# Attention and a gated feed-forward layer on one core: w_out of the first tile loaded and multiplied by column halves

## The chip, the cores and the metric

One core of a Trainium2 chip runs the whole program. The metric is device time in microseconds (us); lower is better. The core has five engines that run beside each other, each through its own instructions in order: TensorE (PE) multiplies, VectorE (DVE) and ScalarE (ACT) do elementwise work and empty PSUM, GpSimd (POOL) works on SBUF only, and SyncE (SP) mostly issues loads. ACT and POOL can issue transfers too. All transfers are carried by 16 DMA engines. Matmul results land in PSUM, which has eight banks of 512 float32 columns on 128 partitions.

## The reference

Blockwise causal attention over 8 batches, 8 heads, 576 positions and head size 64, then a gated feed-forward layer over the 4608 tokens:

```
mask = pos[:, None] // 64 >= pos[None, :] // 64
scores = np.where(mask, q @ k.T / 8, -1e9)
attn = softmax(scores) @ v                       # q, k, v: (8, 8, 576, 64)
x = attn.transpose(0, 2, 1, 3).reshape(4608, 512)
out = (np.maximum(x @ w_gate, 0) * (x @ w_val)) @ w_out   # 512 -> 1536 -> 512
```

The inputs are float32; the kernel multiplies in bfloat16 and gives float32.

## The kernel before, in words

**Tiles.** The feed-forward layer runs in nine tiles of 512 tokens: tile j below 8 is the first 512 positions of batch j, and tile 8 gathers the last 64 positions of all batches. A tile has an up part (gate and value products against `wg` and `wv`, each kept as three blocks of 512 hidden columns; relu on ACT; the product `hT` on DVE) and an output part (`hT` against `wo`). Tiles 0 and 1 take the plain output: four groups of 128 tokens, each 12 matmuls of 512 columns (`out_mm`). Later tiles use a scheme of seven products per 2x2 block (`seven_products`, matmuls of 256 columns).

**Attention.** A pair of heads is a round r = 4 b + hp. Each round has named steps: `s` the scores (`visit`, two double banks "sc" and two single banks of `thirds`) with their first exponentials on ACT, `e` the last exponential, `c` the corners (`corners`: memsets that zero what the block mask forbids), `a` and `b` the products with v of its two heads (`head_av`, with the division on DVE), and `x` the transposes into the tile's input xT. Before that, batch 1's q and k are cast (`q4`, `q6` for heads 4 to 7) and transposed on PE (`m0` to `m3`, `mains_1`). Batch 0 has its own form: `p` (a part of the scores with its exponential), `M` (transposes of q and k), `c0` to `c3b`, `a`, `b`, `x`.

**Order.** The order is written out by hand. `ffn_gen` is a generator that yields after each of the feed-forward layer's matmuls (or pairs of them); the table `AT` gives each other step a place, counted in those yields. Places 0 to 96 are tile 0's up part, 96 to 144 its output part, 144 begins tile 1. Steps are issued in the order of their places, and every engine then runs its share in that order. `HOW` says which engine or PSUM bank a step uses. Loads with places below those of their casts go to SP's queue in the same order: `w00` to `w21` load w_out, `cw..` cast it on POOL; `E1v0` loads v of heads 0 to 3 of batch 1 (casts `ev0a`, `ev0b`), `E1v4` that of heads 4 to 7 (cast `ev4`, L223), `E1q4` and `E1q6` its q and k; `T0`, `E2q0` and later ones follow. A load needs a free one of ten "stage" buffers, each of 4 KB on a partition. The casts turn float32 into bfloat16.

**PSUM.** "sc" has two double banks, "one" a single bank, "ffnp" three banks; a buffer is taken again when its reader is done. In tile 0's output part the four groups rotate through the "ffnp" banks. Each result is copied to an "ob" buffer on DVE (L1191), and its store is kept for later (`late`, issued at steps `o0` to `o3`).

Of the kernel before, what the change touches and what calls it, by code (L numbers as in the profile page):

```python
# [10 lines left out]
FP = mybir.dt.float32  # L11
BF = mybir.dt.bfloat16
# [5 lines left out]
def kernel(  # L18
# [10 lines left out]
    nc = tc.nc  # L29
# [17 lines left out]
    sb = ctx.enter_context(tc.tile_pool(name="sb", bufs=1))  # L47
# [320 lines left out]
    def load_w(dst, view):  # L368

        st = new_stage(1024).rearrange("p (c n) -> p c n", c=dst.shape[1])  # L370
        nc.sync.dma_start(st, view.rearrange("(c p) f -> p c f", p=128))
        return dst, st
# [14 lines left out]
        )  # L387

    def load_w_out(i, g):
        return load_w(  # L390
            wo[i][:, 2 * g : 2 * g + 2],
            moe_w_out[512 * i + 256 * g : 512 * i + 256 * g + 256],
        )

    def cast_w(w, eng, rows=slice(None)):
        dst, st = w
# [36 lines left out]
    def head_of(hh):  # L433
        return slice(64 * hh, 64 * hh + 64)

    def thirds():
        return (
            psum_one.tile([128, 512], FP, name="one"),
            psum_ffn.tile([128, 512], FP, name="ffnp"),
        )  # L440

    def visit(r):

        b, hp = divmod(r, 4)
        at = attnT[r % 4]
        first = psum_sc.tile([128, 2, 512], FP, name="sc")
        second = psum_sc.tile([128, 2, 512], FP, name="sc")
        third = thirds()
        tails = b >= FIRST
        pieces = [(2, False), *((c, True) for c in range(4) if tails)]  # L450
        for c, tail in pieces + [(c, False) for c in (0, 1, 3)]:
            for hh in range(2):
                where = {
                    0: first[:, hh, :],
                    1: second[:, hh, 0:384],
                    3: second[:, hh, 384:512],
                    2: third[hh][:, 0:256],
                }
                if tail:
                    o = third[hh][:, 256 + 64 * c : 320 + 64 * c]  # L460
# [481 lines left out]
    def ffn_gen():  # L942
        for j in range(B + 1):
# [245 lines left out]
            def finish(op, s, n0, n1):  # L1189
                ob = sb.tile([128, 512], FP, name="ob", bufs=5)[:, 0 : n1 - n0]  # L1190
                nc.vector.tensor_copy(ob, op)  # L1191
                if store:
                    store.pop()()
                (store if j else late).append(lambda j=j: put(j, s, ob, n0, n1))

            if j >= SEVEN:
                sums.step(12)
                yield from seven_products(j, quads, sums)
                continue

            groups = outs(j)
            while groups:
                some = 2 if j == 0 and len(groups) == 4 else 1
                ops = [
                    psum_ffn.tile([128, 512], FP, name="ffnp")[:, 0 : n1 - n0]
                    for _, n0, n1 in groups[:some]
                ]
                for f0 in (0, 4, 8) if some == 2 else (0,):
                    for op, (s, n0, n1) in zip(ops, groups):
                        for f in range(f0, f0 + 4 if some == 2 else 12):  # L1210
                            out_mm(op, s, f, n0, n1)
                            if f == 11:
                                finish(op, s, n0, n1)
                            yield
                groups = groups[some:]

    def outs(j):
        full = [(s, 0, 512) for s in range(4)]
        return full if j < B else full[:3] + [(3, 0, 352), (3, 352, 512)]
# [26 lines left out]
    with tc.manual_schedule(engines={E.PE, E.DVE, E.Activation, E.Pool, E.SP}):  # L1246
# [81 lines left out]

        def mains_1(hp):
            engs, banks = HOW[f"m{hp}"]  # L1330
            if banks == "one":
                both = bank("one", BF)
# [5 lines left out]
        AT = {  # L1338
            "p00": -41,
            "p02": -40.5,  # L1340
            "cq4": -40,
# [10 lines left out]
            "p12": -34.5,  # L1352
            "j2": -34,
            "M3q": -33.5,
            "M3k": -33,
            "cv0": -32.5,
            "cv2": -32,
            "c1": -31.5,
            "p20": -31,
            "a0": -30.5,  # L1360
            "p21": -30,
            "b0": -29.5,
# [4 lines left out]
            "x0": -27,  # L1367
            "cv00/01": -26.5,
            "cv00/23": -26,
            "cg00/01": -25.5,  # L1370
            "p30": -25,
            "cv4a": -24.5,
            "cv4b": -24,
            "cg00/23": -23.5,
            "x1": -23,
            "p32": -22.5,
            "c2": -22,
            "c3a": -21.5,
            "c3b": -21,
            "cv6a": -20.5,  # L1380
            "a2": 3,
            "b2": 3.01,
            "cv6b": 3.02,
            "C1": 3.03,
            "a3": 6,
            "b3": 6.01,
            "x2": 6.02,
            "x3": 8,
            "g01": -53.5,
            "v01": -53.4,  # L1390
# [16 lines left out]
            "cv20": 31,  # L1407
            "cg21": 31.91,
            "cv21/0": 32.24,
            "ev0a": 32.33,  # L1410
            "ev0b": 32.34,
            "Lq0": -63.5,
            "Lq2": -62.27,
            "Lv0": -61.59,
# [12 lines left out]
            "j1": -41.2,  # L1427
            "j4": -41.17,
            "E1q0": 20.29,
            "w01": 32.1,  # L1430
            "w00": 32.11,
            "w11": 32.11,
            "w20": 32.12,
            "w10": 32.12,
            "E1v0": 32.16,
            "w21": 32.16,
            "E1q6": 32.19,
            "E1q4": 32.19,
# [5 lines left out]
            "cw00": 32.3,  # L1444
            "cw10": 32.3,
            "cw01": 32.3,
            "cw21/0": 32.33,
            "cw11": 32.33,
            "cw20": 32.33,
            "q6": 32.36,  # L1450
            "q4": 32.36,
            "E2q4": 33.82,
            "ev4": 34.05,
            "tc0": 34.05,
# [5 lines left out]
            "m1": 87.1,  # L1460
            "s4": 95,
            "E2v0": 109.09,
            "cw21/1": 110.84,
            "e4": 114.3,
            "c4": 116.83,
            "s5": 119.48,
            "a4": 120.37,
            "b4": 120.57,
            "e5": 121.28,
            "m2": 122.6,  # L1470
            "c5": 124.67,
            "E2v4": 125.35,
            "T2": 126.26,
            "a5": 127.05,
            "s6": 128.09,
            "e6": 128.35,
            "b5": 129.8,
            "c6": 131.42,
            "m3": 132.5,
            "x4": 135.4,  # L1480
            "x5": 135.8,
            "s7": 139.49,
            "a6": 139.55,
            "b6": 140.59,
            "e7": 141.27,
            "c7": 141.68,
            "x6": 145.48,
            "a7": 147.62,
            "b7": 147.81,
            "x7": 153,  # L1490
            "td0": 156.81,
            "t0": 163.43,
            "td1": 157,
# [89 lines left out]
            "t1": ("dve", "dve"),  # L1583
            "m0": (("act", "dve"), "one"),
            "m1": (("dve", "act"), ("sc", "ffn")),
            "m2": (("act", "act"), ("sc", "ffn")),
            "m3": (("act", "act"), "one"),
            "u0": ("pool", "pool"),
            "u3": ("dve", "act"),
            "r4": ("dve", "one", "ffn", ("act", "sc")),  # L1590
            "r5": ("dve", "ffn", "ffn", ("act", "ffn")),
            "r6": ("dve", "ffn", "ffn", ("act", "sc")),
            "r7": ("dve", "sc", "one", ("dve", "one")),
# [9 lines left out]
            "cw21/1": "dve",  # L1603
            "cv00/01": "pool",
            "cg01/01": "pool",
            "c0": "dve",
            "c1": "dve",
            "c2": "dve",
            "c3a": "dve",
            "c3b": "dve",  # L1610
            "M1": ("dve", "dve"),
            "M2": ("dve", "dve"),
            "M3": ("dve", "dve"),
# [7 lines left out]
            "cw21/0": "pool",  # L1621
            "cg00/01": "pool",
            "cg00/23": "pool",
            "cg01/23": "act",
# [21 lines left out]
                "c" + n: piece(n)  # L1646
                for n in (
                    "g00/01 g00/23 v00/01 v00/23 g01/01 g01/23 v01 g10 v10 g11 v11 "
                    "g20 v20 g21 v21/0 v21/1 w00 w01 w10 w11 w20 w21/0 w21/1"
                ).split()  # L1650
            },
            "C0": lambda: constants(0, nc.vector),
# [162 lines left out]
```

## Time and profile before

| | us |
|---|---|
| median of 3 runs (351.25 to 351.93) | 351.65 |
| the profiled execution | 352.3 |
| its span, first to last instruction | 350.5 |
| PE busy | 339.8 (97%) |
| DVE, ACT, POOL busy | 225.5, 185.2, 153.8 |
| granted TensorE clock | 0.999 |

The rest of the profile is read in the prediction. A group or timeline row gives the start, the busy time, the engine, the line of the kernel, the operation, out<-in with shapes, and in brackets how long the engine stood idle before it and what released it. "SPq" or "ACTq" is an engine's sequencer, which issues transfers. The chain of waits goes back from the last instruction, at each step to what released it. A table by stage gives the engines' busy times, the clock, the share of time that a DMA engine moved data (packets that overlap can bring it over 1), and GB/s.

### The profile page before, as it was taken

What the parts mean: (1) busy time and instruction counts of PE and PEld (TensorE: products, weight loads), DVE (VectorE), ACT (ScalarE), POOL (GpSimd) and SP (SyncE); (2) the same over time, 40 slices, a digit from 0 to 9 for tenths busy, and PEclk for the clock granted to TensorE, in tenths of its full rate; (3) what the DMA queues carried; (4) which work ended last, traced back from release to release, by engine and by line L of the source; (5) the groups of instructions that cost most, each with busy time, mean ns of one, the idle gap of its engine ahead of it and who ended that gap; (6) DMA issues with size and microseconds to landing.
All of it is one profiled execution on the core that took longest, in us unless ns stands there. A gap on an engine that the chain in (4) does not pass through costs nothing.

```text
span 350.5 us, 8275 instructions
## 1 busy us (share of the span) xinstructions
PE 339.8 (97%) x3210; PEld 208.2 (59%) x3254; DVE 225.5 (64%) x564; ACT 185.2 (53%) x297; POOL 153.8 (44%) x194
## 2 busy tenths in 40 slices
PE   8999999999999999999999999999999999999994
PEld 3544455545445568545855576556755687687673
DVE  4853455667529784467547772668567867986892
ACT  5933766687235862666355545555366525423521
POOL 2767556576598902590149203950300022213213
PEclk9999999999999999999999999999999999999999
DMA  8999989999999994999459974999510031003005
GB/s 240 295 353 373 352 224 248 222 148 155 184 185 153 144 182 98 138 147 169 62 134 141 104 135 123 127 131 150 121 47 17 16 94 50 2 2 121 1 2 120
DMA packets 155399, 50.02 MB, mean 143 GB/s; under 512 B 134464, under 2 KB 151744, under 8 KB 155360
## 3 DMA queue, kind: packets, MB, share of 16 engines
q0 software_dynamic: 70528, 8.98, 49.1%
q1 hardware_dynamic: 77520, 32.52, 44.0%
q10 hardware_dynamic: 7312, 8.00, 7.8%
q8 instruction: 25, 0.41, 0.5%
q14 instruction: 14, 0.11, 0.1%
HBM read 37.75 MB, written 9.44 MB: 135 GB/s over the span
## 4 chain that ended last, share of the span: by engine, by line
PE 77%; DMA 14%; POOL 3%; issue 2%; DVE 2%; ACT 1%; SPq 1%; POOLq 0%; ACTq 0%
PE ffnp L948 39%; PE ffnp L830 12%; PE one L830 5%; PE sc L1014 3%; DMA stage<-in_moe_w_out_dram 3%; PE sc L465 3%; DMA xT<-xnat 2%; DMA stage<-in_moe_w_val_dram 2%; PE one L465 2%; DMA stage<-in_v_dram 2%; DMA stage<-in_moe_w_gate_dram 2%; PE ffnp L600 2%; PE one L600 2%; PE ffnp L1181 2%; PE one L1014 2%
## 5 line engine op out<-in xcount | busy, mean ns | idle before, releaser
L958 ACT ACTIVATE gate_sb<-ffnp 128x512 bf16<-128x512 f32 x95 | 57.1, 605 | 74.8 <-PE ffnp L948 66.5
L948 PE MATMUL ffnp<-xT,wg 128*128 128x512 bf16 x338 | 93.0, 379 | 1.7 <-issue 0.6
L948 PE MATMUL ffnp<-xT,wv 128*128 128x512 bf16 x309 | 87.7, 380 | 1.0 <-DVE hT L968 0.3
L968 DVE TENSOR_TENSOR hT<-gate_sb,ffnp 128x512 bf16<-128x512 bf16 x76 | 51.9, 683 | 46.0 <-PE ffnp L948 27.0
L948 PEld LDWEIGHTS <-wv 128*128 128x128 bf16 x384 | 35.4, 98 | 38.2 <-issue 4.6
L470 ACT ACTIVATE attnT<-sc 128x1024 bf16<-128x1024 f32 x56 | 57.0, 1042 | 0.0
L948 PEld LDWEIGHTS <-wg 128*128 128x128 bf16 x384 | 35.7, 98 | 35.0 <-issue 1.7
L882 POOL TENSOR_TENSOR ob<-ob 128x512 f32<-128x512 f32 x7 | 9.6, 1370 | 101.7 <-ACT ob L879 53.3
L830 PEld LDWEIGHTS <-stage 128*128 128x128 bf16 x420 | 40.3, 98 | 6.0
L789 DVE TENSOR_TENSOR stage<-hT 128x512 bf16<-128x512 bf16 (+2 forms) x82 | 37.8, 493 | 0.9
L600 PEld LDWEIGHTS <-attnT 128*128 128x128 bf16 x640 | 26.7, 98 | 11.9 <-DVE attnT L1241 0.9
L830 PE MATMUL ffnp<-stage 128*128 128x256 bf16 x252 | 31.4, 273 | 0.0
L353 POOL DMA_DIRECT2D v_bf<-in_v_dram x30 | 24.1, 869 | 6.1 <-DVE recip L537 2.6
L477 ACT ACTIVATE attnT<-one 128x512 bf16<-128x512 f32 (+1 forms) x28 | 15.0, 536 | 21.1 <-PE ffnp L465 21.1
L353 POOL DMA_DIRECT2D q_bf<-in_q_dram x20 | 17.9, 907 | 16.7 <-DVE hT L968 9.7
L1181 PE MATMUL ffnp<-wo,hT 128*128 128x512 bf16 x91 | 23.2, 379 | 0.3
L465 PEld LDWEIGHTS <-kTm 64*128 64x128 bf16 x384 | 11.0, 94 | 15.1 <-issue 7.9
L1045 POOL TENSOR_TENSOR ob<-ob 128x512 f32<-128x512 f32 x6 | 7.6, 1266 | 23.2 <-ACT ob L1044 23.2
L353 POOL DMA_DIRECT2D k_bf<-in_k_dram x20 | 17.8, 927 | 0.0
L830 PEld LDWEIGHTS <-hT 128*128 128x128 bf16 x168 | 16.4, 98 | 1.9
L465 PE MATMUL sc<-qTm,kTm 64*128 64x512 bf16 (+1 forms) x168 | 16.8, 305 | 0.0
L879 ACT COPY ob<-ffnp 128x512 f32<-128x512 f32 x7 | 4.1, 585 | 22.1 <-PE ffnp L830 22.1
(194 smaller groups left out, 556.0 us busy)
## 6 DMA issues: line engine op xcount, KB each, us to landing
out_dram<-ob ACTq DMA_DIRECT2D x28, 256.0 KB, 2.3
stage<-in_moe_w_val_dram SPq DMA_DIRECT2D x6, 512.0 KB, 8.7
stage<-in_moe_w_gate_dram SPq DMA_DIRECT2D x6, 512.0 KB, 8.2
stage<-in_moe_w_out_dram SPq DMA_DIRECT2D x6, 512.0 KB, 10.5
q_bf<-in_q_dram POOLq DMA_DIRECT2D x20, 128.0 KB, 4.2
k_bf<-in_k_dram POOLq DMA_DIRECT2D x20, 128.0 KB, 5.2
v_bf<-in_v_dram POOLq DMA_DIRECT2D x20, 128.0 KB, 7.0
stage<-in_v_dram SPq DMA_DIRECT2D x19, 128.0 KB, 5.5
```

The source lines that it names most:

```text
L353: ins = nc.gpsimd.dma_start(dst, part_of)
L465: nc.tensor.matmul(o, kTm[b % 2][head_of(hh), c, hp, :], qT, start=True, stop=True)
L470: return lambda: nc.scalar.activation(at[:, :, lo : lo + 512], sc, AF.Exp, scale=scale)
L477: nc.scalar.activation(at[:, hh, 1024 : 1024 + w], third[hh][:, 0:w], AF.Exp, scale=scale)
L600: nc.tensor.matmul(av[:, p, :], at[:, col : col + 128], v_bf[b % 2][:, c, h, :], start=(p == 0), stop=(c == p), skip_group_check=True,)
L789: nc.vector.tensor_tensor(out=out.rearrange("p (c n) -> p c n", c=m), in0=a, in1=b, op=op)
L830: nc.tensor.matmul(to, sums.of(c)[which][:, 128 * p : 128 * p + 128], right, start=first, stop=(c == 5), skip_group_check=True,)
L948: nc.tensor.matmul(to, (wg, wv)[t][f // 4][:, c, 128 * (f % 4) : 128 * (f % 4) + 128], x[:, c], start=(c == 0), stop=(c == 3),)
L958: nc.scalar.activation(gate_sb, gate, AF.Relu)
L968: nc.vector.tensor_tensor(out=h, in0=gate_sb, in1=val, op=AX.mult)
L1014: nc.tensor.matmul(to[:, 256 * k : 256 * k + 256], left[:, c, 128 * k : 128 * k + 128], right[:, c], start=new and (k, c) == (0, 0), stop= ...
L1181: nc.tensor.matmul(op, hT[f][:, 128 * s : 128 * (s + 1)], wo[f // 4][:, f % 4, n0:n1], start=(f == 0), stop=(f == 11),)
```

## The change

A block of w_out used to be 256 rows of 512 hidden rows, with all 512 columns; now it is all 512 rows with 256 columns, so that each row that the transfer fetches is 1 KB and not 2 KB long. Tile 0's output is computed in four quarters: columns 0 to 255 of token groups 0 and 1, then of groups 2 and 3, then columns 256 to 511 in the same way. A quarter is 24 matmuls of 256 columns into the bank "one", one yield for each two, then a copy to an "ob" buffer and a late store (`put_block`). Tile 1 is as it was.

SP issues the three left halves of w_out, then `E1v0`, `E1q4`, `E1q6`, then the three right halves, then `E1v4`. Batch 1's visits take fixed places among the quarters: `s5`, `a4`, `m2`, `b4` after the first quarter (108), `s6`, `m3`, `a5`, `b5` in the second (114), `s7` and `x4` at its end (120), `a6`, `b6`, `x5` in the third (122), `a7`, `b7` (126), `x6` (129), and `x7` (133). The bank pairs of batch 1's `thirds` are both "ffn", as are the banks of `m2`, `m3`, `a`, `b` and `x` of rounds 4 to 7; `m2` and `m3` are emptied on DVE and no longer on ACT, and `x4` on DVE, `x5` and `x6` on ACT, `x7` on DVE.

In batch 0, the corners c1, c2 and c3b are zeroed on POOL and no longer on DVE; the scores p20 stand before the transposes M3k; c2 comes earlier, cg00/23 later, and b2, a3, x2, b3 change places by a few yields.

```diff
     def load_w_out(i, g):
-        return load_w(
-            wo[i][:, 2 * g : 2 * g + 2],
-            moe_w_out[512 * i + 256 * g : 512 * i + 256 * g + 256],
-        )
+        n = slice(256 * g, 256 * g + 256)
+        return load_w(wo[i][:, :, n], moe_w_out[512 * i : 512 * i + 512, n])
...
-    def thirds():
-        return (
-            psum_one.tile([128, 512], FP, name="one"),
-            psum_ffn.tile([128, 512], FP, name="ffnp"),
-        )
+    def thirds(r):
+        return [bank("ffn" if i or r // 4 == 1 else "one") for i in range(2)]
...
-            groups = outs(j)
+            for half, s0 in [(h, s) for h in range(2) for s in (0, 2)] if j == 0 else []:
+                op = bank("one")
+                order = [
+                    (f, s)
+                    for i in range(3)
+                    for s in (s0, s0 + 1)
+                    for f in range(4 * i, 4 * i + 4)
+                ]
+                for n, (f, s) in enumerate(order):
+                    nc.tensor.matmul(
+                        op[:, 256 * (s - s0) : 256 * (s - s0) + 256],
+                        hT[f][:, 128 * s : 128 * (s + 1)],
+                        wo[f // 4][:, f % 4, 256 * half : 256 * half + 256],
+                        start=(n == 0),
+                        stop=(f == 11),
+                        skip_group_check=True,
+                    )
+                    if n == 23:
+                        ob = sb.tile([128, 512], FP, name="ob", bufs=5)
+                        nc.vector.tensor_copy(ob, op)
+                        late.append(
+                            lambda s0=s0, half=half, ob=ob: put_block(
+                                0, s0 // 2, 256 * half, ob, 0, 2
+                            )
+                        )
+                    if n % 2:
+                        yield
+            groups = outs(j) if j else []
...
+            "w00": 32.1,
+            "w10": 32.101,
+            "w20": 32.102,
+            "E1v0": 32.11,
+            "E1q4": 32.12,
+            "E1q6": 32.13,
+            "w01": 32.14,
+            "w11": 32.141,
+            "w21": 32.142,
...
+            "e4": 95.1,
+            "c4": 108,
+            "s5": 108.01,
+            "e5": 108.02,
+            "a4": 108.03,
+            "m2": 108.04,
+            "b4": 108.05,
+            "s6": 114,
+            "e6": 114.01,
+            "c5": 114.02,
+            "m3": 114.03,
+            "a5": 114.04,
+            "b5": 114.05,
+            "s7": 120,
+            "e7": 120.01,
+            "x4": 120.02,
+            "c6": 120.03,
+            "a6": 122,
+            "b6": 122.01,
+            "x5": 122.02,
+            "c7": 126,
+            "a7": 126.01,
+            "b7": 126.02,
+            "x6": 129,
+            "x7": 133,
...
-            "s5": 119.48,
-            "a4": 120.37,
...
-            "a6": 139.55,
-            "b6": 140.59,
...
-            "x7": 153,
...
-            "m2": (("act", "act"), ("sc", "ffn")),
-            "m3": (("act", "act"), "one"),
+            "m2": (("dve", "dve"), "ffn"),
+            "m3": (("dve", "dve"), "ffn"),
...
-            "r4": ("dve", "one", "ffn", ("act", "sc")),
+            "r4": ("dve", "ffn", "ffn", ("dve", "ffn")),
...
-            "c1": "dve",
-            "c2": "dve",
+            "c1": "pool",
+            "c2": "pool",
             "c3a": "dve",
-            "c3b": "dve",
+            "c3b": "pool",
```

More of the change, by code (lines that the diff above doesn't have):

```diff
@@ L447, in visit @@
         second = psum_sc.tile([128, 2, 512], FP, name="sc")
-        third = thirds()
+        third = thirds(r)
         tails = b >= FIRST
@@ L1193, in finish @@
                     store.pop()()
-                (store if j else late).append(lambda j=j: put(j, s, ob, n0, n1))
+                store.append(lambda j=j: put(j, s, ob, n0, n1))
             if j >= SEVEN:
@@ L1199, in ffn_gen @@
                 continue
-            groups = outs(j)
-            while groups:
[L1203 to L1215, printed above, removed]
+            for half, s0 in [(h, s) for h in range(2) for s in (0, 2)] if j == 0 else []:
[26 more added lines that the diff above has]
+            groups = outs(j) if j else []
+            while groups:
+                s, n0, n1 = groups.pop(0)
+                op = psum_ffn.tile([128, 512], FP, name="ffnp")[:, 0 : n1 - n0]
+                for f in range(12):
+                    out_mm(op, s, f, n0, n1)
+                    if f == 11:
+                        finish(op, s, n0, n1)
+                    yield
     def outs(j):
@@ L1330, in mains_1 @@
             engs, banks = HOW[f"m{hp}"]
-            if banks == "one":
-                both = bank("one", BF)
+            if isinstance(banks, str):
+                both = bank(banks, BF)
                 two = [both[:, 512 * t : 512 * t + 512] for t in range(2)]
@@ L1338 @@
         AT = {
+            "w00": 32.1,
[7 more added lines that the diff above has]
+            "w21": 32.142,
+            "cw00": 32.3,
+            "cw10": 32.301,
+            "cw20": 32.302,
+            "ev0a": 32.33,
+            "ev0b": 32.331,
+            "q4": 32.34,
+            "q6": 32.35,
+            "cw01": 32.36,
+            "cw11": 32.361,
+            "cw21": 32.362,
+            "e4": 95.1,
[23 more added lines that the diff above has]
+            "x7": 133,
             "p00": -41,
@@ L1354 @@
             "M3q": -33.5,
[L1355 to L1359, printed above, removed]
+            "p20": -33,
+            "M3k": -32.5,
+            "cv0": -32,
+            "cv2": -31.5,
+            "c1": -31,
             "a0": -30.5,
@@ L1369 @@
             "cv00/23": -26,
[L1370 to L1374, printed above, removed]
+            "c2": -25.5,
+            "cg00/01": -25,
+            "p30": -24.5,
+            "cv4a": -24,
+            "cv4b": -23.5,
             "x1": -23,
             "p32": -22.5,
-            "c2": -22,
-            "c3a": -21.5,
+            "c3a": -22,
+            "cv6a": -21.5,
             "c3b": -21,
-            "cv6a": -20.5,
+            "cg00/23": -20.5,
             "a2": 3,
-            "b2": 3.01,
+            "b2": 4,
+            "a3": 6,
+            "b3": 6.02,
+            "x2": 6.01,
             "cv6b": 3.02,
             "C1": 3.03,
-            "a3": 6,
-            "b3": 6.01,
-            "x2": 6.02,
             "x3": 8,
@@ L1409 @@
             "cv21/0": 32.24,
-            "ev0a": 32.33,
-            "ev0b": 32.34,
             "Lq0": -63.5,
@@ L1429 @@
             "E1q0": 20.29,
[L1430 to L1438, printed above, removed]
             "E1v4": 32.19,
@@ L1443 @@
             "q0": 32.24,
[L1444 to L1451, printed above, removed]
             "E2q4": 33.82,
@@ L1462 @@
             "E2v0": 109.09,
-            "cw21/1": 110.84,
-            "e4": 114.3,
-            "c4": 116.83,
-            "s5": 119.48,
-            "a4": 120.37,
[L1468 to L1471, printed above, removed]
             "E2v4": 125.35,
             "T2": 126.26,
[L1474 to L1482, printed above, removed]
-            "a6": 139.55,
-            "b6": 140.59,
[L1485 to L1489, printed above, removed]
-            "x7": 153,
             "td0": 156.81,
@@ L1585 @@
             "m1": (("dve", "act"), ("sc", "ffn")),
-            "m2": (("act", "act"), ("sc", "ffn")),
-            "m3": (("act", "act"), "one"),
+            "m2": (("dve", "dve"), "ffn"),
+            "m3": (("dve", "dve"), "ffn"),
             "u0": ("pool", "pool"),
             "u3": ("dve", "act"),
-            "r4": ("dve", "one", "ffn", ("act", "sc")),
+            "r4": ("dve", "ffn", "ffn", ("dve", "ffn")),
             "r5": ("dve", "ffn", "ffn", ("act", "ffn")),
-            "r6": ("dve", "ffn", "ffn", ("act", "sc")),
-            "r7": ("dve", "sc", "one", ("dve", "one")),
+            "r6": ("dve", "ffn", "ffn", ("act", "ffn")),
+            "r7": ("dve", "ffn", "ffn", ("dve", "ffn")),
             "r8": ("dve", "one", "ffn", None),
@@ L1602 @@
             "cv21/1": "dve",
-            "cw21/1": "dve",
             "cv00/01": "pool",
@@ L1620 @@
             "r3": ("one", "sc", "dve", "sc"),
-            "cw21/0": "pool",
             "cg00/01": "pool",
@@ L1648 @@
                     "g00/01 g00/23 v00/01 v00/23 g01/01 g01/23 v01 g10 v10 g11 v11 "
-                    "g20 v20 g21 v21/0 v21/1 w00 w01 w10 w11 w20 w21/0 w21/1"
+                    "g20 v20 g21 v21/0 v21/1 w00 w01 w10 w11 w20 w21"
                 ).split()
```

## The prediction

> **What bounds the kernel now.** First the page's busy shares and slices, to see which engine has no slack:
>
> ```profile
> PE 339.8 (97%) x3210; PEld 208.2 (59%) x3254; DVE 225.5 (64%) x564; ACT 185.2 (53%) x297; POOL 153.8 (44%) x194
> ...
> PE   8999999999999999999999999999999999999994
> ```
>
> TensorE is full in every slice but the first and the last. A busy PE need not be at its peak, so I read the spacing of its matmuls: 0.2155 us for 512 columns almost everywhere. Spaces of twice that fit missing records (3254 weight loads, 3210 matmuls). Between 20 us and the end only a few real waits are left; the largest between 40 and 60 us is the one below. So work that is merely moved on PE costs nothing, and a new wait on PE is paid in full.
>
> The change lies in the first 60 us, so next the stage of tile 0's output, and PE where those matmuls end:
>
> ```profile
> 40.65:58.13 17.48, 17.10 (x171) 9.49 (x171) 8.16 (x26) 12.85 (x23) 10.84 (x15) 1.00 0.97 245
> ```
>
> ```profile
> 55.41 0.46 PE L600 MATMUL ffnp<-v_bf,attnT 128*128 128x65 bf16 x10
> 55.71 0.38 PE L1181 MATMUL ffnp<-wo,hT 128*128 128x512 bf16 x1
> ```
>
> The stage's columns are PE, PEld, DVE, ACT, POOL, then granted clock, DMA share and GB/s: the clock is whole, and the DMA engines (0.97) are as full as PE. The 55.41 row is a6, the first product of batch 1 with head 4 of v. PE is 0.3 us late for it, and the chain of waits says why:
>
> ```profile
> 46.85 6.95 DMA stage<-in_v_dram
> 54.30 1.07 POOL v_bf L223
> 55.41 0.46 PE ffnp L600 x10
> ```
>
> Last, GpSimd in order of time. Its casts start when a load lands, so their starts are a clock for the loads:
>
> ```profile
> 24.35 1.04 POOL L397 CAST wv<-stage 128x1024 bf16<-128x1024 f32 x1 [0.47 <-DMA stage<-in_moe_w_val_dram]
> 25.85 1.04 POOL L397 CAST wg<-stage 128x1024 bf16<-128x1024 f32 x1 [0.46 <-DMA stage<-in_moe_w_gate_dram]
> ...
> 28.70 1.04 POOL L397 CAST wg<-stage 128x1024 bf16<-128x1024 f32 x1 [0.31 <-DMA stage<-in_moe_w_gate_dram]
> 30.03 1.04 POOL L397 CAST wv<-stage 128x1024 bf16<-128x1024 f32 x1 [0.30 <-DMA stage<-in_moe_w_val_dram]
> ...
> 34.27 1.04 POOL L198 CAST q_bf<-stage 128x1024 bf16<-128x1024 f32 x1 [0.89 <-DMA stage<-in_q_dram]
> 38.46 2.02 POOL L397 CAST wo<-stage 128x1024 bf16<-128x1024 f32 x2 [3.15 <-DMA stage<-in_moe_w_out_dram]
> ...
> 45.85 0.62 POOL L231 CAST v_bf<-stage 128x512 bf16<-128x512 f32 x1 [0.26 <-DMA stage<-in_v_dram]
> 46.52 0.61 POOL L198 CAST q_bf<-stage 128x512 bf16<-128x512 f32 x1
> 47.21 0.61 POOL L198 CAST k_bf<-stage 128x512 bf16<-128x512 f32 x1
> 49.41 0.61 POOL L198 CAST q_bf<-stage 128x512 bf16<-128x512 f32 x1 [1.59 <-DMA stage<-in_q_dram]
> 50.27 0.61 POOL L198 CAST k_bf<-stage 128x512 bf16<-128x512 f32 x1 [0.25 <-DMA stage<-in_k_dram]
> 54.30 1.06 POOL L223 CAST v_bf<-stage 128x1024 bf16<-128x1024 f32 x1 [3.41 <-DMA stage<-in_v_dram]
> ```
>
> A 512 KB weight block in rows of 1 KB (column halves) takes 1.50 us (24.35 to 25.85), in rows of 2 KB 1.35 (28.70 to 30.03). The second half of batch 1's v (54.30) closes this run of loads.
>
> **The change, part by part.** I follow one quantity: when PE has done everything from 40.65 us on that both programs do, namely tile 0's output and batch 1's visits with their transposes. Before: a6 starts at 55.41, PE leaves the output at 57.09, and x6 (0.22), a7 and b7 (0.60) and x7 (0.22), which stand among tile 1's matmuls, bring it to 58.13.
>
> *The split matmuls.* 48 of 512 columns become 96 of 256. The seven-product stage runs 256-column matmuls, each with its own weight load, 8 in 0.87 us (0.109 each): 96 x 0.109 - 48 x 0.2155 = +0.12 us. By the Trainium skill (TensorE: Matmul & The Clock Gate, Back-to-back issue gap) sustained spacing is about 81 ns at 128 and 131 ns at 512 columns; 98 ns at 256, an estimate between them, would give 96 x 0.098 - 48 x 0.131 = +3.1 us. The trace disagrees with that rule at 0.2155 us for 512 columns.
>
> *The loads.* SP now issues three w_out halves, v of heads 0 to 3, q and k of heads 4 to 7, three w_out halves, v of heads 4 to 7. Before, all six w_out blocks came first. The bytes ahead of the last v are the same, but a w_out half has 1 KB rows. From q at 34.27 and its k 1.5 us later (35.75) the clock of after runs: three halves 4.5, to 40.25; v 1.87 (the DVE w_out cast at 43.98 to 45.85), to 42.1; four q/k; three halves 4.5; v again. The four q/k took 4.42 (45.85 to 50.27) with a pause in them; at the pace of 46.52 to 47.21 they take 2.76. The last v took 4.03 (50.27 to 54.30), or 1.87 at the pace of the first. So its cast starts between 51.25 and 55.07; on GpSimd's queue the last three w_out casts (1.04 each) now stand before it, but they start as their blocks land 1.5 us apart and are done by then. Both pauses come where v's small rows queue, and that queue is still there, but three large blocks now stand before the last v and may fill one pause: I take the middle, 53.2. With the cast (1.06) and 0.05 to PE, a6 can start at 54.3 (52.4 to 56.2).
> By the Trainium skill (DMA: Bandwidth & Descriptors, Specifications) rows from 512 B on run at line rate, so 1 KB rows would cost what 2 KB rows do: 6 x 0.15 = 0.9 us less, a6 at 53.4. The two spacings above disagree with it.
>
> *When PE wants a6.* Tile 0's first quarter finds its three halves cast in time (the third lands at 40.25, is needed at 42.6), and q and k of heads 4 to 7 land earlier than before, for m2 and m3. The visits move up: a6 goes from place 139.55 to 122, ahead of 44 of the 96 half matmuls. From 40.87: 24 halves 2.62, s5 0.75 (46.06 to 46.80), a4 0.31, m2 0.45, b4 0.31, 12 halves 1.31, s6 0.75, m3 0.45, a5 and b5 0.61, 12 halves 1.31, s7 0.75, x4 0.22, 4 halves 0.44: a6 is due at 51.2. DVE could make it later, since it takes over m2's and m3's four copies (0.65 each, from ACT): copy of the first quarter 0.69 from 43.7, corners 0.33, a4 0.62, m2 1.3, b4 0.62, corners 0.33, m3 1.3, a5 and b5 1.24, copy of the second quarter 0.69 make 50.8, plus waits in between of up to 1 us. The third quarter needs that copy, so a6 is due between 51.2 and 52.3. The load is later at nearly every value of its range: PE waits about 3 us at a6, with everything queued behind it.
>
> *After a6.* a6 and b6 0.61, x5 0.22, 8 halves 0.87, a7 and b7 0.61, 6 halves 0.65, x6 0.22, 6 halves 0.65, x7 0.22, 24 halves 2.62: 6.67 us. One wait is new. All four quarters use the single bank "one", and between the third and the fourth no other matmul stands. A copy to ob starts 0.04 us after its last matmul (47.19 to 47.23) and takes 0.69; with 0.27 for that matmul and 0.05 back to PE, less a slot of 0.109, it is 0.95 us (0.9 to 1.15 if DVE answers late). Before, three rotating banks hid this copy.
>
> *Batch 0's start.* Five corner memsets (0.165 each on DVE) go to GpSimd, where the row of that shape says 0.306: 1.5 us more, before and between weight casts that still end ahead of their matmuls, since GpSimd idled 0.78 before the 19.89 cast and its constants fill that. Scores p20 step ahead of M3k, where ACT idled 0.42 us. The later visits still wait for v (cast 15.83 to 16.24), so I expect 0.2 us less on PE (between 0 and 0.9, what PE waits there). While a load decides a6, this gain ends in a6's wait. It moves no load, since the loads follow each other without a gap from 20 us on. Costed at nothing also: x4 and x7 on DVE, thirds in two "ffn" banks, and stores in 1 KB rows, all beside other work; if that cover went, each would be a few tenths.
>
> *Sum.* PE is through at 54.3 + 6.67 + 0.95 = 61.9 against 58.13: +3.8 us. Nothing later gives it back, since PE has no waits left to give. The profiled execution took 352.3 us (span 350.5 and 1.8 around it); the median is 0.65 lower, and I take it: 351.65 + 3.8 = 355.45.
>
> **Rivals.**
> *The load comes early enough, and the banks decide.* For: 51.25 is possible if both pauses go. Then 0.95 for the single bank, 0.12, up to 1.1 for DVE's queue, less a6's old 0.3 and 0.2 at the start: +0.6 to +1.7, about 352.8.
> *Faster.* PE is through before 58.13 if a6 starts before 50.5, so if the v cast starts before 49.4. That is 1.9 us ahead of the load's best pace, so the small rows of v would have to travel beside the large w_out blocks (the DMA share over 1 in places speaks for some of it), and DVE's 50.8 would have to shrink as well. With a cast at 48.9 it is -0.5: 351.15. Against it is that every landing in the clock is late, not early.
> *The loads get worse.* The three late halves run into the tail loads behind them and a third pause of about 2 us follows: 357.5 to 358.5.
>
> **How the numbers follow.** Load decides 0.70 (a6 at 52.4 to 56.2: +1.9 to +5.7, 353.5 to 357.4); banks decide 0.15; loads worse 0.07; faster 0.06; between them, no change, 0.02. This kernel can tell 0.2%, 0.7 us, from no change; the banks' case is beyond that save its edge, so 0.01 goes to no change: faster 0.06, same 0.03, slower 0.91. The range takes in the banks' middle and the first part of the worse case: 352.7 to 358.0.
>
> **What would show it.** PE stands still for 2 to 5 us before the first product with head 4 of v, released by GpSimd's v cast (L223), which starts at 51 to 55 us behind a DMA; the fourth quarter's first matmul waits some 0.95 us for the DVE copy; 256-column output matmuls 0.109 apart; ACT without its gap near 11.4 us. From 62 us on the old trace shifted as a whole. I am wrong if the v cast starts before 50, or if PE finds waits later on that swallow the loss.

## The result, and the profile after

The changed kernel takes 357.97 us in the median of six runs (355.86 to 358.3), against 351.48 us (351.25 to 351.93) for the kernel before on the same chip: a ratio of 1.0175, with a 95% interval of 1.015 to 1.02. The change costs 6.5 us. The forecast was 355.45, 3.8 us more than before.

The execution that was profiled is the shortest of the six, 355.86 us (span 354.1, granted clock 1.0). The other five lie at 357.62 to 358.3, with a mean clock of 0.995. Why is the question of the experiments. First the page of the changed kernel, its busy shares and slices:

```profile
PE 343.5 (97%) x3302; PEld 213.6 (60%) x3302; DVE 225.9 (64%) x563; ACT 182.7 (52%) x292; POOL 156.4 (44%) x199
...
PE   8999987999999999999999999999999999999994
```

A slice is 8.85 us long, and besides the first and the last, TensorE now has two that are not full, the sixth and the seventh, from 44.3 to 62 us, where tile 0's output stands. The stage from 40.65 us to the end of the fourth quarter, in the table by stage (PE, PEld, DVE, ACT, POOL, granted clock, DMA share, GB/s), is now 21.91 us long, where it was 17.48, and PE is busy for 18.24 of them:

```profile
40.65:62.56 21.91, 18.24 (x238) 14.56 (x234) 11.61 (x34) 10.90 (x18) 13.34 (x19) 1.00 1.07 280
```

PE's rows in this stage show where it stands still (L1205 are the quarter matmuls, L595 the products with v):

```profile
51.70 0.61 PE L1205 MATMUL one<-wo,hT 128*128 128x256 bf16 x4
54.64 0.76 PE L595 MATMUL ffnp<-v_bf,attnT 128*128 128x65 bf16 x20 [2.33 <-POOL v_bf L223]
...
58.12 0.82 PE L1205 MATMUL one<-wo,hT 128*128 128x256 bf16 x6
59.72 0.38 PE L1205 MATMUL one<-wo,hT 128*128 128x256 bf16 x2 [0.78 <-DVE ob L1215]
...
60.16 2.56 PE L1205 MATMUL one<-wo,hT 128*128 128x256 bf16 x22
```

The row at 54.64 is a6, which waits for the cast of v of heads 4 to 7. The row at 59.72 is the fourth quarter's first matmul, which waits for the DVE copy that empties the single bank. The brackets count from an end that is modelled; by the spacing of the matmuls the two waits are 2.50 and 0.94 us. The chain of waits names what a6 waits for:

```profile
47.40 5.98 DMA stage<-in_v_dram
...
53.52 1.07 POOL v_bf L223
...
54.64 0.47 PE ffnp L595 x10
```

And GpSimd's rows, the clock of the loads, from the last k of batch 1 on:

```profile
45.41 0.62 POOL L198 CAST k_bf<-stage 128x512 bf16<-128x512 f32 x1 [0.17 <-DMA stage<-in_k_dram]
47.21 1.04 POOL L395 CAST wo<-stage 128x1024 bf16<-128x1024 f32 x1 [1.18 <-DMA stage<-in_moe_w_out_dram]
48.81 1.04 POOL L395 CAST wo<-stage 128x1024 bf16<-128x1024 f32 x1 [0.56 <-DMA stage<-in_moe_w_out_dram]
51.21 1.04 POOL L395 CAST wo<-stage 128x1024 bf16<-128x1024 f32 x1 [1.36 <-DMA stage<-in_moe_w_out_dram]
53.52 1.06 POOL L223 CAST v_bf<-stage 128x1024 bf16<-128x1024 f32 x1 [1.27 <-DMA stage<-in_v_dram]
```

The three right halves of w_out start 1.60 and 2.40 us apart, and v follows 2.31 us later. So the two waits that were forecast are there, at the places named. What the profiled execution does not show is why five of six runs take some 2 us more.

### The profile page after: what moved, and what is told of

It is laid out like the page before. It is cut to its first block, busy times and chain, and to the rows that moved or that the text cites. A ratio compares the mean times of both kernels' runs of the same rounds, so it can differ in the third digit from the quotient of the medians.

```text
span 354.1 us, 8425 instructions
## 1 busy us (share of the span) xinstructions
PE 343.5 (97%) x3302; PEld 213.6 (60%) x3302; DVE 225.9 (64%) x563; ACT 182.7 (52%) x292; POOL 156.4 (44%) x199
## 4 chain that ended last, share of the span: by engine, by line
PE 81%; DMA 11%; SPq 2%; POOL 2%; DVE 2%; issue 1%; ACT 0%; POOLq 0%
PE ffnp L943 41%; PE ffnp L825 11%; PE one L825 5%; DMA stage<-in_moe_w_val_dram 4%; DMA stage<-in_v_dram 4%; PE sc L1009 3%; PE ffnp L1176 3%; PE sc L460 3%; DMA stage<-in_moe_w_gate_dram 2%; SPq L162 2%; PE one L460 2%; PE ffnp L595 2%; PE one L1009 2%; PE one L595 2%; PE one L1205 1%; PE ffnp L557 1%
## 5 line engine op out<-in xcount | busy, mean ns | idle before, releaser
L943 PE MATMUL ffnp<-xT,wg 128*128 128x512 bf16 x356 | 95.9, 379 | 0.0
L943 PE MATMUL ffnp<-xT,wv 128*128 128x512 bf16 x328 | 90.9, 380 | 0.0
L595 PEld LDWEIGHTS <-attnT 128*128 128x128 bf16 x640 | 26.7, 98 | 14.0 <-issue 2.7
L472 ACT ACTIVATE attnT<-one 128x512 bf16<-128x512 f32 (+1 forms) x24 | 13.5, 561 | 16.6 <-PE ffnp L460 13.7
L472 ACT ACTIVATE attnT<-ffnp 128x512 bf16<-128x512 f32 (+1 forms) x32 | 16.0, 514 | 3.2 <-PE ffnp L460 3.2
```

Of the source, the lines that this page charges most:

```text
L472: nc.scalar.activation(at[:, hh, 1024 : 1024 + w], third[hh][:, 0:w], AF.Exp, scale=scale)
L595: nc.tensor.matmul(av[:, p, :], at[:, col : col + 128], v_bf[b % 2][:, c, h, :], start=(p == 0), stop=(c == p), skip_group_check=True,)
L943: nc.tensor.matmul(to, (wg, wv)[t][f // 4][:, c, 128 * (f % 4) : 128 * (f % 4) + 128], x[:, c], start=(c == 0), stop=(c == 3),)
```

## The experiments

The theory after the result: PE's standstill at a6 sets the loss, the single bank adds its 0.95 us, and in most runs a third cost comes on top that the shortest run escapes. Candidates for the third are a lowered TensorE clock behind the standstill, and v landing later. The rivals within the sum are the bank, the early place of the visits, the order of the loads, and batch 0's new start.

**e1: the changed kernel again, unaltered,** for a profile of an execution that is not the shortest.

> The changed kernel as it is, for a second profile. Its first profile spanned 354.1 us at a granted clock of 1.00; five other runs spanned about 356.3 at 0.995. Theory A: the standstill of TensorE at a6 (2.5 us in the first profile) is longer in most runs, and after it the clock is granted lower for some us, which costs the other 2 us: a profile at 0.995 shows a stretch of low clock just after a6, matmuls of that stretch spaced about twice as far, and the rest at full speed. Rival B: the 2 us come from somewhere else (a later load, a wait behind tile 1, or all matmuls a little slower): the stretch after a6 then looks as in the first profile and the loss is spread or elsewhere. Time 355.8 to 358.3 by both.

Measured: 357.69 us (357.28 to 358.39, four runs), ratio 1.018 (1.0165 to 1.0195). The profiled execution took 357.28. PE's rows behind the standstill:

```profile
51.56 0.61 PE L1205 MATMUL one<-wo,hT 128*128 128x256 bf16 x4
54.73 0.99 PE L595 MATMUL ffnp<-v_bf,attnT 128*128 128x65 bf16 x20 [2.56 <-POOL v_bf L223]
...
55.94 1.91 PE L1205 MATMUL one<-wo,hT 128*128 128x256 bf16 x8
...
61.13 0.38 PE L1205 MATMUL one<-wo,hT 128*128 128x256 bf16 x2 [0.78 <-DVE ob L1215]
```

a6 starts 0.09 us later than in the first profile, but eight quarter matmuls now take 1.91 us. In the first profile the same eight took 1.04. From a6 to the fourth quarter it is 6.40 us instead of 5.08: +1.32. The table by stage shows the cause in its clock column (the figure ahead of the DMA share). The changed kernel's first profile, and then e1:

```profile
55.10:58.50 3.40, 3.27 (x56) 2.82 (x53) 2.54 (x10) 0.76 (x2) 1.82 (x4) 1.00 1.20 291
```

```profile
51.69:55.10 3.41, 0.84 (x17) 0.65 (x16) 0.60 (x3) 1.50 (x2) 2.17 (x3) 1.00 0.88 202
55.10:58.51 3.41, 3.41 (x42) 2.92 (x39) 1.50 (x7) 0.58 (x1) 1.44 (x4) 0.50 1.14 292
```

The clock record of e1's trace is whole up to 55.10 us, at 0.50 for 3.413 us, and whole again. So the third cost is a lowered clock, in one stretch of 3.413 us, that begins 0.37 us after PE has resumed. 3.41 us at half clock could lose 1.7 us of work; 1.3 arrive. A part falls into time that PE had lost anyway, such as the 0.29 us that a7 waits for its corners in the first profile.

**e9 and e10: the changed kernel twice more,** run last, one execution each. In e1 the half clock begins 15 times 3.413 us after the record's first entry: the record changes on a grid. These two runs ask whether the place of the grid decides.

> The changed kernel once more, unaltered. Theory (the grid): the clock record changes on a grid of 3.413 us that lies at another place in each execution; if one grid window holds about 2.4 us or more of the standstill at a6, the next window is granted 0.5 and the time is 357.2 to 358.4; if the standstill is spread over two windows, the clock stays whole and the time is about 355.9. Rival (length alone): a standstill of over 2.6 us brings the low window wherever the grid lies, a shorter one does not. The v cast is expected between 53.4 and 55.5 us, as in the executions so far.

> The changed kernel once more, unaltered: a further place of the grid for the same standstill. Grid theory: low window and 357.2 to 358.4 if one grid window holds about 2.4 us or more of the standstill, else whole clock and about 355.9. Rival: the length of the standstill alone decides, from about 2.6 us. The v cast at 53.4 to 55.5 us.

Measured: 358.68 and 358.93 us, both above the 357.2 to 358.4 that were expected with a low window, since a6 started later than in e1. The v casts start at 54.92 and 55.28, as expected. The table by stage on each trace's own grid, first the changed kernel's first profile, then e9, then e10:

```profile
50.04:53.46 3.42, 2.22 (x21) 1.38 (x19) 2.27 (x7) 2.67 (x5) 1.04 (x1) 1.00 0.92 179
53.46:56.87 3.41, 2.10 (x40) 1.75 (x40) 1.42 (x6) 0.59 (x1) 2.48 (x5) 1.00 0.97 299
```

```profile
50.43:53.84 3.41, 1.95 (x19) 1.18 (x17) 2.03 (x7) 2.49 (x4) 1.55 (x2) 1.00 0.70 145
53.84:57.26 3.42, 1.22 (x28) 1.19 (x28) 0.69 (x3) 0.20 (x1) 2.27 (x4) 1.00 1.04 286
57.26:60.67 3.41, 3.41 (x34) 2.71 (x33) 1.86 (x8) 0.39 (x1) 1.13 (x3) 0.50 1.28 220
```

```profile
52.93:56.34 3.41, 0.00 (x0) 0.00 (x0) 0.00 (x0) 0.37 (x1) 1.55 (x3) 1.00 0.88 212
56.34:59.75 3.41, 3.35 (x35) 2.82 (x35) 1.43 (x6) 0.59 (x1) 2.34 (x5) 0.50 1.18 292
```

Each row is one window of the grid; the first figure after its length is PE's busy time. Set beside PE's standstill (its matmul starts):

| execution | standstill at a6 | its share in one grid window (the next) | clock of the window after | a6 | time |
|---|---|---|---|---|---|
| after, first profile | 2.50 | 1.32 (1.18) | 1.0 (1.0) | 54.64 | 355.86 |
| e1 | 2.73 | 2.73 (0) | 0.5 | 54.73 | 357.28 |
| e9 | 3.77 | 1.57 (2.20) | 1.0 (0.5) | 56.04 | 358.68 |
| e10 | 4.29 | 0.82 (3.41) | 1.0 (0.5) | 56.40 | 358.93 |
| e4 (below) | 3.69 | 0.85 (2.84) | 1.0 (0.5) | 55.59 | 357.23 |

In e9 the half clock begins 1.22 us after PE has resumed, at the next line of the grid, and the window with 1.57 us of standstill brought none. So the grid decides when the clock falls. The mark lies between 1.77 us of standstill in one window (e2 below) and 2.20; I had expected it at 2.4. The five rows alone would leave room for the rival (length alone, a mark somewhere between 2.50 and 2.73), since no short standstill fell into one window whole. The ends of the traces decide it. Behind the last matmul of the program the clock falls at a line of the grid too. In e9 this is 2.19 us after that matmul's time was up (2.02 after its modelled end):

```profile
350.80:354.21 3.41, 1.39 (x13) 1.00 (x11) 1.51 (x3) 0.00 (x0) 1.65 (x2) 1.00 0.89 209
354.22:356.81 2.59, 0.00 (x0) 0.00 (x0) 0.00 (x0) 0.00 (x0) 0.00 (x0) 0.50 0.28 88
```

In e3 it is 2.34 us, in e4 2.48. At the lines that came 1.33 us or less behind the last matmul (1.33 in e1, 1.10 in the first profile) the clock stayed whole for one window more. So 2.2 us in one window are enough, where the first profile's 2.50 in two windows were not, and length alone is ruled out.

The times follow from two numbers, when a6 starts and whether the clock falls. 355.86, plus what a6 is later than 54.64, plus 1.32 for the half clock gives 357.27 for e1, from which the 1.32 is taken (measured 357.28), 358.58 for e9 (358.68) and 358.94 for e10 (358.93). From a6 to the fourth quarter it is 6.40 us in e9 and 6.36 in e10, as in e1.

**e2: work for PE in the standstill.** Nine matmuls on zeros into a bank that nobody reads, ahead of a6.

```diff
+    def junk_sc(n):
+        to = bank("sc")
+        for _ in range(n):
+            nc.tensor.matmul(to, zeros[:, 0:128], zeros, start=True, stop=True)
...
+            "jw": 121.5,
```

> The changed kernel with nine matmuls of 512 columns on zeros put before a6, into an 'sc' bank that nobody reads, so that TensorE works while it waits for v. The wait for v itself stays. Theory A (a lower clock follows the standstill): the clock stays at 1.00 in all runs and the time is that of the best runs, 355.5 to 356.3. Rival B (the 2 us have another cause): the median stays near 358.0. If the wait at a6 were shorter than the nine matmuls (1.9 us), both would be slower by what sticks out; the profile tells.

Measured: 356.74 us (356.13 to 357.88, four runs), ratio 1.0145 (1.0128 to 1.0162), 0.95 less than e1, though 0.4 above the upper end of what was expected. No run has a mean clock under 0.997, where all four of e1 have 0.995. The profiled execution is the slowest of the four. Its clock stays whole to the end of the matmuls, but v came late (cast at 55.44):

```profile
52.62 2.10 PE L1256 MATMUL sc<-zeros 128*128 128x512 bf16 x8 [0.38 <-ACT attnT L465]
...
56.55 0.76 PE L595 MATMUL ffnp<-v_bf,attnT 128*128 128x65 bf16 x20 [1.61 <-POOL v_bf L223]
...
57.38 1.04 PE L1205 MATMUL one<-wo,hT 128*128 128x256 bf16 x8
```

```profile
54.67:58.08 3.41, 1.80 (x34) 1.56 (x32) 0.96 (x4) 0.50 (x1) 2.36 (x4) 1.00 1.07 308
58.08:61.50 3.42, 2.65 (x40) 2.07 (x38) 2.19 (x8) 0.67 (x2) 1.04 (x1) 1.00 1.28 196
```

By the spacing PE still stands for 1.77 us before a6, all in the first of these two windows of the grid, and the second has the whole clock. The eight quarter matmuls take 1.04 us again. The two numbers hold here too: 355.86 + (56.55 - 54.64) = 357.77, without a clock term (measured 357.88). Useless work in the hole thus keeps the clock whole and saves its 1.3 us, and nothing of the wait itself.

**e3: v of heads 4 to 7 loaded ahead of the right halves.**

```diff
-            "E1v4": 32.19,
+            "E1v4": 32.135,
...
-            "ev4": 34.05,
+            "ev4": 32.355,
```

> The changed kernel, but v of heads 4 to 7 is loaded and cast before the right halves of w_out instead of behind them. Theory (the load of v decides a6): the v cast starts near 48 instead of 53.5, a6 waits for nothing, the right halves come some 2 us later and still in time; the profile gets 2.3 to 2.5 us shorter, 353.2 to 353.8, and the clock stays at 1.00. Rival (DVE's queue or the bank sets a6): a6 stays within 0.5 us of 54.6 and the time at 355.9 or above. Rival (the right halves become the late ones): a wait of 1 to 2 us moves to the third or the fourth quarter, 354.5 to 355.8.

Measured: 353.75 us (353.68 to 354.9, four runs), ratio 1.0073 (1.0057 to 1.009). In the profiled execution (354.9) v's cast starts at 48.40 and a6 waits for nothing. The right halves are late in its place, as the second rival had it, though by less:

```profile
52.40 0.60 PE L1205 MATMUL one<-wo,hT 128*128 128x256 bf16 x4 [0.62 <-POOL wo L395]
...
56.72 0.38 PE L1205 MATMUL one<-wo,hT 128*128 128x256 bf16 x2 [0.67 <-POOL wo L395]
```

So the order of the loads moves the wait and cuts it, from 2.5 to 4.3 us in one piece to 0.78 and 0.83 in two by the spacing (0.20 of the first is a wait for DVE that the first profile has too), too short for the clock. It does not remove it; that this is because the same bytes stand in the same queue is argued and was not varied.

**e4: the fourth quarter in one of the "sc" banks,** all else as changed.

```diff
-                op = bank("one")
+                op = bank("sc" if (half, s0) == (1, 2) else "one")
```

> The changed kernel, but the fourth quarter goes into an 'sc' bank instead of waiting for the copy of the third in 'one'. Theory: the wait of 0.94 us between the third and the fourth quarter is gone and nothing else changes: 0.9 to 1.0 us less than the changed kernel at the same clock (354.9 in a run at 1.00, near 357.0 in a run at 0.995). Rival: the wait comes back at the beginning of tile 1 or at x7 (DVE still has the copy to do), and the time stays within 0.3 us of the changed kernel.

Measured: 356.85 us (355.0 to 357.23, four runs), ratio 1.0143 (1.0115 to 1.0171). The wait before the fourth quarter is gone:

```profile
60.39 0.82 PE L1205 MATMUL one<-wo,hT 128*128 128x256 bf16 x6
61.04 0.38 PE L1205 MATMUL sc<-wo,hT 128*128 128x256 bf16 x2
```

The median is 0.84 below e1's, but the two sets of runs nearly touch (357.23 and 357.28), and v's landing scatters (a6 waits 3.69 us in this profile). The bank's price is measured better where a6 doesn't wait, in the next pair.

**e5: the visits of rounds 6 and 7 moved behind the fourth quarter's start; e6: the same with the bank of e4.**

```diff
-            "a6": 122,
-            "b6": 122.01,
+            "a6": 140,
+            "b6": 140.01,
...
-            "a7": 126.01,
-            "b7": 126.02,
-            "x6": 129,
-            "x7": 133,
+            "a7": 142,
+            "b7": 142.01,
+            "x6": 143,
+            "x7": 143.5,
```

> The changed kernel, but a6, b6, a7, b7, x6 and x7 stand in the fourth quarter (places 140 to 143.5) instead of the third and fourth (122 to 133). The loads are untouched. Theory (a6 was moved ahead of its data): a6 is due near 56 us, after its v cast (53.5 to 55.4 so far), so TensorE no longer stands still and no window of low clock follows; the wait between third and fourth quarter stays: 353.2 to 354.2 in all runs, at clocks of 0.997 to 1.00. Rival (the loads are slower by themselves and TensorE waits for something else that lands late): a wait of over 1 us stays somewhere between 50 and 62 us, and the time at 355 or above.

> The same late visits, and the fourth quarter in an 'sc' bank. Theory: both new waits are gone, 0.9 to 1.0 us less than with late visits alone: 352.2 to 353.3. What is then left over the kernel before (0.7 to 1.8 us) is DVE's queue (a4 behind the copy and the corners, 0.45 us), 0.12 us for the split matmuls and the start. Rival: the two waits overlap, and it is no faster than late visits alone.

Measured: e5 353.75 us (353.68 to 353.97), ratio 1.0063 (1.0048 to 1.0077); e6 352.88 us (352.45 to 353.08), ratio 1.0037 (1.0024 to 1.005), four runs each. PE's rows of e5, then of e6:

```profile
55.62 1.91 PE L1205 MATMUL one<-wo,hT 128*128 128x256 bf16 x16 [0.78 <-DVE ob L1215]
```

```profile
54.72 1.91 PE L1205 MATMUL sc<-wo,hT 128*128 128x256 bf16 x16
...
59.31 0.40 PE L636 MATMUL ffnp<-ident,xnat 128*128 128x128 bf16 x4 [0.59 <-DVE xnat L534]
```

With a6 back at about its old place (139.55), the standstill is gone, and 3.9 us with it (357.69 to 353.75). The bank is then worth 0.87 us (353.75 to 352.88). What e6 still loses lies in small waits: 0.55 before a4, 0.75 before x7, which follows x6 too closely for DVE's division, and 0.2 each before x4 and the third quarter.

**e11: e3 and e4 together,** v first and the fourth quarter in "sc".

> v of heads 4 to 7 ahead of the right halves, and the fourth quarter in a double bank sc. Theory: the two causes add: 353.75 with v first, less the 0.9 us of the single bank (which also cost 0.87 between the two kernels with late visits): 352.9 (352.6 to 353.3), since PE would wait 0.6 each at the first matmuls on the right halves but not before the fourth quarter. Rival: with the bank's wait gone PE comes earlier to the last right half's cast, and waits there instead: 353.5 to 353.8.

Measured: 353.15 us (352.79 to 353.87, four runs), ratio 1.0047 (1.0029 to 1.0066), 0.60 less than e3 by the medians. The sum held in its range; in the profiled execution (353.23) the wait for the last right half is still there, as the rival had it, but short:

```profile
55.96 0.38 PE L1205 MATMUL one<-wo,hT 128*128 128x256 bf16 x2 [0.18 <-POOL wo L395]
```

**e7: e6 with batch 0's start as before, and batch 1's first corners ahead of the first copy on DVE** (`c4` from 108 to 107.5), to take away a4's wait.

> The same again, with the start of batch 0 as in the kernel before (corners on DVE, old order) and c4's corners ahead of the first quarter's copy on DVE. Theory: a4 no longer waits for the corners, 0.4 us less than the run before it, 351.8 to 352.8; the start gives or costs at most 0.2. Rival: the wait moves from a4 to the next step on DVE's queue (m2's copies before s6), and nothing is gained.

Measured: 353.23 us (352.72 to 354.33, six runs), ratio 1.0051 (1.0036 to 1.0065): no gain on e6, and above the range that was expected. a4 no longer waits, and in the profiled execution, the slowest of the six, the time is lost again further on:

```profile
56.59 0.76 PE L595 MATMUL ffnp<-v_bf,attnT 128*128 128x65 bf16 x20 [0.32 <-POOL v_bf L223]
...
66.22 0.41 PE L498 MATMUL sc<-qTt,kTm 64*128 64x64 bf16 x16 [0.96 <-DVE hT L963]
```

PE arrives earlier and finds v's cast (at 55.48 here) not done even at the late place of a6, and DVE's queue not emptied at 66 us. Whether the faster runs of e7 lose their time at the same places is not shown.

**e8: the kernel before with batch 0's new start alone** (the corners on POOL, p20 ahead of M3k, the moved places).

> The kernel before, with the start of batch 0 alone changed (corners c1, c2, c3b on GpSimd, p20 ahead of M3k, the small moves). Theory: since the visits that follow wait for v and a6 then for its load, nothing is gained or lost: 351.3 to 351.7, first matmul of s4 within 0.2 us of 40.0. Rival (the memsets on GpSimd delay weight casts): 0.2 to 0.9 us slower, with a wait of TensorE on a GpSimd cast before 25 us. Rival (ACT's gap closed is a gain): s4 0.2 to 0.5 us earlier, but the time no more than 0.1 us shorter, since a6 still waits for v.

Measured: 351.49 us (351.24 to 352.07, eleven runs) against 351.42 (seventeen runs): ratio 1.0001 (0.9992 to 1.0009). This part does nothing to the time. Its profile (351.3 us, span 349.5) lists no wait of PE between 20 and 120 us (two spaces of 0.31 us, at 62.9 and 68.8, stand in the profile of before too), unlike the kernel before as it was profiled. There, the start of tile 2 waited for a transpose by DMA, which the chain of waits shows:

```profile
94.75 8.70 DMA xT<-xnat
...
103.50 0.39 PE ffnp L948
...
107.33 0.61 DVE hT L968
...
107.98 2.32 PE ffnp L948 x10
```

PE lost 0.21 us there, and 0.43 at 107.98, where it waited for DVE. Together with a6's 0.30 that is 0.94 of the 1.0 us by which the profile of before exceeds e8's (352.3 against 351.3).

Against e8 all losses add up. The waits of over 0.1 us by the spacing of the matmuls, summed over the stage, and 0.12 for the split matmuls (e11's 0.28 at a6 is a wait for its corners on DVE, not for v):

| kernel | a4 | a6 | bank | others | sum with 0.12 | its profiled time less 351.3 |
|---|---|---|---|---|---|---|
| after, first profile | 0.54 | 2.50 | 0.94 | 0.66 | 4.76 | 4.56 |
| e3 | 0.54 | 0 | 0.95 | 2.08 (right halves 0.78, 0.83) | 3.69 | 3.60 |
| e5 | 0.54 | 0 | 0.95 | 1.12 (x7 0.75) | 2.73 | 2.67 |
| e6 | 0.55 | 0 | 0 | 1.12 (x7 0.75) | 1.79 | 1.78 |
| e11 | 0.54 | 0.28 | 0 | 1.02 | 1.96 | 1.93 |

No kernel run here is faster than the one before: with both large waits gone, e6 still pays 1.8 us in its profile (1.5 by the medians), nearly all of it in small waits, most of them on DVE.

## Why the prediction was right and wrong

*The split matmuls, +0.12 us:* right. The fourth quarter's 22 matmuls in a row take 2.56 us by their modelled end, 0.109 apart, and the sums above close with 0.12. The rule of the Trainium skill that was weighed against it (TensorE: Matmul & The Clock Gate, Back-to-back issue gap) does not hold here: 256 and 512 columns took 0.109 and 0.2155 us in long rows, as before.

*Batch 0's start, 0.2 us less on PE:* not there in the time. The gap of 0.42 us on ACT near 11.4 us did close, but e8 shows that nothing comes out of it, to within 0.3 us.

*When PE wants a6, 51.2 to 52.3 us:* right, PE was ready at 52.14 in the first profile. DVE's queue was the cause, as the upper end had it: the third quarter starts at 51.70, 0.05 us after the copy of the second.

*The loads: the last v's cast at 53.2, between 51.25 and 55.07.* The bounds were nearly right, the middle was too early. The casts of v started at 53.52, 53.62, 54.92 and 55.28 in the four profiles of the changed kernel, at 54.48 in e4 and at 55.44 in e2. Set beside the terms of the sum, from one cast's start to the next:

| term | forecast | first profile | e1 | e9 | e10 |
|---|---|---|---|---|---|
| second cast of v of heads 0 to 3, at | 42.1 | 42.85 | 42.83 | 42.53 | 42.90 |
| to the last of the four q/k | 2.76 to 4.42 | 2.56 | 3.89 | 3.22 | 3.32 |
| to the third right half | 4.5 | 5.80 | 4.62 | 5.99 | 6.16 |
| to the last v | 1.87 to 4.03 | 2.31 | 2.28 | 3.18 | 2.90 |

The two terms with a pause came below their middle (3.59 and 2.95) in three of the four profiles each, so "I take the middle" was a fair guess for them. The term that was mis-sized is "three halves 4.5" for the right halves, the one that was charged at the pace of 1.50 without a range: it took 0.1 to 1.7 us more. In three of the four, gaps opened among these blocks themselves: their casts start 1.60 and 2.40 us apart in the first profile, 1.98 and 1.84 in e9, 1.61 and 3.09 in e10. Another 0.4 to 0.8 us were lost before all this. Together v's cast is late by 0.3 to 2.1 us. If the median run of 357.97 had the half clock, as three of the four profiles do, a6 stood at some 55.4 in it (357.97 - 355.86 - 1.32 = 0.79 behind 54.64) and not at 54.3.

*After a6, 6.67 us and a new wait of 0.95:* right. In the first profile PE is through at 62.56, 7.92 after a6, 0.3 more than forecast, which a7 waits for its corners on DVE. The new wait was 0.94, and its removal brought 0.87 between e5 and e6.

*"PE waits about 3 us at a6, with everything queued behind it":* the length was right (2.5 to 4.3), the price was not. The sum charged the standstill at its length. In three of the four profiles it also cost 1.3 us of half clock behind it. This is the term that was missing, and e2 shows it by taking it away. The forecast's +3.8, the median's later a6 (+1.1) and the clock (+1.3) make 6.2 of the 6.5 us. The Trainium skill has the rule that should have been a rival here (TensorE: Matmul & The Clock Gate, Why this matters for your kernels): no idle gaps of over about 3 us between bursts of matmuls, else the clock falls to half. The same page (What's actually happening) puts it down to a free-running window of 3413 ns. The traces agree with the window, 3.413 us on a grid that lies elsewhere in each execution, and with the half clock. They differ in the mark: windows with 2.20 and 2.73 us of standstill out of 3.41 were enough.

*"Nothing later gives it back":* right, against the median. Set beside before's own profile it looks wrong, since the shift of 4.24 us at 74 us is only 3.61 from 110 us on. But the 0.64 between them are the two waits that this one execution of before had at tile 2, and that e8's profile does not have; against e8 the shift stays at 4.60 from 73 to 152 us.

*The rivals.* "The load comes early enough" needed a cast near 51.25 and did not come about in any profile of the changed order; e3, where v came early by another order, took 353.75 and not 352.8, because the right halves are late then. Its cast at 48.40 was even ahead of the 49.4 that the rival "Faster" asked for, and the kernel was still slower than before; an early v with the right halves in time as well was not run. "The loads get worse" named 357.5 to 358.5 us, where most runs ended, but not for its reason alone: gaps of up to 1.7 us did open among the right halves, but a6 stood at 54.64 to 56.40 in the four profiles, where the rival's times ask for 56.4 to 57.4. The half clock, which was in no term, makes up the rest. So it is largely luck that the median of 357.97 lies inside the range, 0.03 us from its end: that end was there for this rival, and the load's own part of the range stopped at 357.4.

What stays open: why the same loads land up to 2 us apart from run to run (v's cast at 53.5 to 55.4), and what part of their lateness is due to the 1 KB rows (0.9 us by the forecast's two spacings); no run changed the rows without the order.

## What to carry to other kernels

Price a wait on TensorE by its length, and ask what the clock does behind it: here standstills of 2.7 to 4.3 us cost another 1.3 us each, while one of 2.5 over two windows and one of 1.77 in one window cost nothing behind them. Before a consumer is moved forward, look at the clock of its load: the stage gained nothing from the earlier places of rounds 6 and 7 (a6 17.5 yields earlier) and lost 3.9 us by them, as e5 shows. And one profile is one execution: take its time against the other runs' first, for here the profile of after was the one run of six whose mean clock shows no such window, and the profile of before had waits of 0.9 us that e8's, of a kernel with the same time, does not have.

## What the runs showed of the hardware

Behind a standstill that is long enough the granted clock is at 0.50 for exactly one window of 3.413 us, and it falls at a line of a grid: 0.06 us before PE resumed work in e10, 0.37 after in e1, 1.22 after in e9. The grid's first line lay 3.90, 5.14, 5.67 and 6.06 us after the start of the four profiles of the changed kernel. The clock also falls behind the last matmul of the program, at no cost. The mean clock of a run tells the two apart: half of 3.41 us over 355 is 0.0048, and of the thirteen profiled executions the four with such a window in the middle (e1, e4, e9, e10) have means of 0.992 to 0.995, the nine without it 0.997 (e3) to 1.000. So the five first runs at 0.995 very likely had one, though they left no trace.

SP was held for 5.53 us in issuing v's four pieces in the first profile, and the last of them landed 5.98 us after its issue (the chain above). SP's row:

```profile
43.28 5.53 SPq L162 DMA_DIRECT2D stage<-in_v_dram  x4
```

How far this, and not the bytes ahead, sets the landing of v was not tried.
